# A decode kernel that streams its caches: another start address for values and weights, and a reordered last key step

## The chip, the cores and the metric

The kernel runs on one core of a Trainium2 chip. The metric is the device time of one execution in microseconds; lower is better. Before the change the median of three runs is 195.03 us (194.61 to 195.13). A profiled execution has a span of 192.2 us from its first to its last instruction.

A core has five engines that run beside each other: TensorE (PE in the profile, with its weight loads as PEld), VectorE (DVE), ScalarE (ACT), GpSimd (POOL) and SyncE (SP). Each runs its own instructions in order and waits for the others through semaphores. Sixteen DMA engines move data between the chip's memory (HBM) and the on-chip memory (SBUF), which has 128 partitions. TensorE writes into PSUM.

## The reference

One token goes through attention over a sliding window of cached keys and values, and through a gating branch. Cut to what matters:

```python
x  = layernorm(A_x)                          # (1, 1, 512)
q  = (x @ wq).reshape(32 heads, 128)
k  = k_cache[:, last 4096]                   # 32 heads x 4096 x 128, bf16
v  = v_cache[:, last 4096]
p  = softmax(q . k * 128 ** -0.5)            # per head, over 4096 positions
s  = concat(p @ v) @ wo                      # (4096,) @ (4096, 512)
# gating branch on the same x: g = silu(x1 + gelu(layernorm(x1) @ w3) @ w4),
# where x1 = x + hs, and hs = shifted(h) @ w2 is zero for one token
out = A_x + s * g
```

Every key and every value is used once, for one query. So there is little arithmetic per byte: 32 MiB of K and 32 MiB of V are read, and with the weights the profile counts 79.02 MB.

## The kernel before

The heads go through in eight groups of four (`G = 4`). A group's K is one tile of 128 partitions by 32,768 bytes (4 MiB), and so is its V. Step `s` works on the keys of group `s` and on the values of group `h = s - 2`; steps 8 and 9 have values only.

Memory in a partition is handed out pool after pool, in 32-byte units, so that what is allocated first sets the start of what follows:

```python
k_pool = ctx.enter_context(tc.tile_pool(name="k", bufs=K_BUFS))       # 3 tiles of 32 KiB
kt_pool = ...; prod_pool = ...
const = ctx.enter_context(tc.tile_pool(name="const", bufs=1))         # neg_half lies here
small = ctx.enter_context(tc.tile_pool(name="small", bufs=1))
ps_misc = ctx.enter_context(tc.tile_pool(name="ps_misc", bufs=1, space=PSUM))   # one PSUM bank
ps_tr = ctx.enter_context(tc.tile_pool(name="ps_tr", bufs=3, space=PSUM))
# ... other PSUM pools, and sm_pool for the softmax's small tiles
small.tile([P, 96], BF16, name="pad")
wts_guard = tc.tile_pool(name="wts", bufs=1)    # wq, w2, w3, w4; given up at step 2
# at step 2, in the same place:
v_pool = ctx.enter_context(tc.tile_pool(name="v", bufs=V_BUFS))       # 2 tiles of 32 KiB
wo_blk[2] = v_pool.tile([P, 4, D], BF16, tag="wo_4", bufs=1, name="wo_4")
wo_rows = v_pool.tile([P, H - h_part, D], BF16, tag="wo_rows", bufs=1, name="wo_rows")
# at step 5, in one of the three K buffers:
wo_24 = k_pool.tile([P, 32, D], BF16, tag="kv", name="wo_24")
```

As compiled, the three K tiles start at bytes 16,512, 49,280 and 82,048 of a partition, wq at 151,680, w2 at 184,448, w3 at 188,544, w4 at 199,552, and the two V tiles at 159,872 and 192,640. All of these are 128 more than a multiple of 256. The constant `neg_half` starts at 130,208.

The scores of a group are computed in two ways at once. VectorE multiplies 64 or 80 of the 128 key columns by the query and sums (`k_vector`, four parts). The others go over TensorE: `keys(b0, b1)` turns batches of eight columns (`k_turn`: four transposes, and a copy by ScalarE) and multiplies them by the query (`k_scores`). Then the maximum is taken, and the exponentials:

```python
def sm_max(g):      # VectorE: gather the scores, maximum of each partition
    nc.vector.tensor_reduce(out=s["S"][:, n:CP], in_=s["own"][:, 0:CP - n, :], axis=AX.X, op=ALU.add)
    nc.vector.tensor_reduce(out=s["m1"][:], in_=s["S"][:], axis=AX.X, op=ALU.max)

def sm_turn(g):     # TensorE turns the maxima into a row (in ps_misc); VectorE reduces it
    nc.tensor.transpose(mt_ps[:], s["m1"][:], ident_f[:])
    nc.vector.tensor_reduce(out=mx[:], in_=mt_ps[:].rearrange(...), axis=AX.X, op=ALU.max)
    nc.vector.tensor_scalar(out=md[0:1, :], in0=mx[:], scalar1=-scale, ...)

def sm_exp(g):      # TensorE spreads it to all partitions (ps_misc); ScalarE: four exponentials
    nc.tensor.matmul(mb_ps[:], lhsT=par_t[:]..., rhs=md[:], start=True, stop=True)
    nc.scalar.copy(out=mb[:], in_=mb_ps[:])
    for a in range(G):
        nc.scalar.activation(out=s["pT"][:, :, a], in_=s["S"][:], func=ACT.Exp, scale=scale,
                             bias=mb[:, a:a + 1], accum_out=s["sum"][:, a:a + 1])
```

The values: `v_wide` multiplies a group's V by its weights (32 matmuls, then a copy to SBUF by ScalarE), `v_turn` turns the result (four transposes, in ps_misc, or in ps_tr for the last group), `v_add` and `v_out` sum it and divide by the denominator (VectorE). Then the output projection, in blocks of 16, 8, 4 and 4 heads: `ox_spread` and `ox_pick` bring a block into the form that `y_wide` needs. `y_open` takes a ps_tr bank and clears it, and `y_wide` multiplies the heads by the rows of wo.

The engines' programs in the last steps, in order:

```python
            # step 7 (last keys)
            k_vector(s, kn, 0); keys(0, 2)
            v_turn(h - 1); v_add(h - 1); v_out(h - 1)
            k_vector(s, kn, 1); keys(2, 4)
            sm_den(h); sm_rden(h)
            keys(4, nb - 1)                 # nb is 8 here
            sm_turn(s - 1)
            keys(nb - 1, nb)
            k_scores(s, nb - 1); sm_own(s)
            k_vector(s, kn, 2)
            v_wide(h, v)                    # h = 5: the sixth V
            sm_exp(s - 1)
            k_vector(s, kn, 3)
            sm_max(s); sm_turn(s)           # the last maximum
            v_turn(h); v_add(h); v_out(h)
            ox_spread(1)
            y_open(); y_wide(0, False)
            # step 8
            ox_pick(1)
            sm_exp(NG - 1)
            y_wide(1, False)
            sm_den(NG - 2); sm_rden(NG - 2)
            v_wide(h, v)                    # h = 6: the seventh V
            # ...
            # step 9: the eighth V, loaded in four parts, used part by part (v_wide, v_part);
            # the last four heads with their own rows of wo (y_head), and the end
```

The loads are issued by SyncE in program order as soon as their buffers are free. The last V goes into the buffer of the sixth, and the last four rows of wo (`wo_rows`) are loaded after it.

Of the kernel before, what the change touches and what calls it, by code (L numbers as in the profile page):

```python
# [8 lines left out]
P = 128  # L9
BF16 = mybir.dt.bfloat16  # L10
FP32 = mybir.dt.float32
ACT = mybir.ActivationFunctionType
ALU = mybir.AluOpType
# [13 lines left out]
def kernel(  # L27
# [14 lines left out]
    nc = tc.nc  # L42
# [20 lines left out]
    const = ctx.enter_context(tc.tile_pool(name="const", bufs=1))  # L63
# [54 lines left out]
    nc.vector.tensor_copy(out=sel[:], in_=ident_bf[:, 0:P:32].unsqueeze(1).to_broadcast([P, PB, G]))  # L118
    ind = const.tile([P, 1], FP32, name="ind")
    nc.vector.tensor_reduce(out=ind[:], in_=ident_f[:, 0:P:32], axis=AX.X, op=ALU.max)  # L120
    neg_half = const.tile([P, 1], FP32, name="neg_half")
    nc.vector.memset(neg_half[:], -0.5)


# [33 lines left out]
    def ln_stats(src_f, tag):  # L158
        ps = ps_misc.tile([P, KC], FP32, tag="misc", name="ln_ps")
        nc.tensor.matmul(ps[:], lhsT=ones_f[:], rhs=src_f, start=True, stop=True)  # L160
        tot = small.tile([P, 1], FP32, name=f"ln_tot_{tag}")
        nc.vector.reduce_sum(out=tot[:], in_=ps[:], axis=AX.X)
        negmean = small.tile([P, 1], FP32, name=f"ln_negmean_{tag}")
        nc.vector.tensor_scalar(out=negmean[:], in0=tot[:], scalar1=-1.0 / D,
                                scalar2=None, op0=ALU.mult)
        xc = small.tile([P, KC], FP32, name=f"ln_xc_{tag}")
        nc.vector.tensor_scalar(out=xc[:], in0=src_f, scalar1=negmean[:], scalar2=None,
                                op0=ALU.add)
        sq = small.tile([P, KC], FP32, name=f"ln_sq_{tag}")
        nc.vector.tensor_tensor(out=sq[:], in0=xc[:], in1=xc[:], op=ALU.mult)  # L170
        ps2 = ps_misc.tile([P, KC], FP32, tag="misc", name="ln_ps2")
        nc.tensor.matmul(ps2[:], lhsT=ones_f[:], rhs=sq[:], start=True, stop=True)
        vtot = small.tile([P, 1], FP32, name=f"ln_vtot_{tag}")
        nc.vector.reduce_sum(out=vtot[:], in_=ps2[:], axis=AX.X)
        rstd = small.tile([P, 1], FP32, name=f"ln_rstd_{tag}")
        nc.vector.tensor_scalar(out=rstd[:], in0=vtot[:], scalar1=1.0 / D,
                                scalar2=LN_EPS, op0=ALU.mult, op1=ALU.add)
        nc.gpsimd.tensor_tensor(out=rstd[:], in0=rstd[:], in1=neg_half[:], op=ALU.pow)
        return xc, negmean, rstd


# [86 lines left out]
    for i, (col, w) in enumerate(terms):  # L268
# [28 lines left out]
                            op=ALU.max)  # L297
# [19 lines left out]
    def k_vector(g, kn, part):  # L317
        m = nd(g) // 4
        rows = slice(m * part, m * part + m)
        prod = prod_pool.tile([P, 20, Dh], BF16, tag="prod", name="prod")  # L320
        nc.vector.tensor_tensor(out=prod[:, 0:m, :], in0=kn[:, rows, :],  # L321
                                in1=q_bc[:, g:g + 1, :].to_broadcast([P, m, Dh]), op=ALU.mult)
        nc.vector.tensor_reduce(out=st[g]["S"][:, rows], in_=prod[:, 0:m, :], axis=AX.X, op=ALU.add)  # L323
# [37 lines left out]
    def sm_max(g):  # L361
        s = st[g]
        n = nd(g)
        nc.vector.tensor_reduce(out=s["S"][:, n:CP], in_=s["own"][:, 0:CP - n, :], axis=AX.X, op=ALU.add)  # L364
        s["m1"] = sm_pool.tile([P, 1], FP32, tag="m1", name="m1")
        nc.vector.tensor_reduce(out=s["m1"][:], in_=s["S"][:], axis=AX.X, op=ALU.max)  # L366
# [11 lines left out]
    def sm_exp(g):  # L378
        s = st[g]
        mb_ps = ps_misc.tile([P, G], FP32, tag="misc", name="mb_ps")  # L380
        nc.tensor.matmul(mb_ps[:], lhsT=par_t[:].rearrange("k b a -> k (b a)"), rhs=md[:], start=True,  # L381
                         stop=True)
        mb = sm_pool.tile([P, G], FP32, tag="mb", name="mb")
        nc.scalar.copy(out=mb[:], in_=mb_ps[:])  # L384
        s["pT"] = sm_pool.tile([P, CP, G], BF16, tag="pT", name="pT")
        s["sum"] = sm_pool.tile([P, G], FP32, tag="sum", name="sum")
# [3 lines that stand above are left out]
# [112 lines left out]
    def y_open():  # L502
        yr[0] = ps_tr.tile([P, KC, P], FP32, tag="pt", name="yr_ps")
        zeros(yr[0][:])
# [18 lines left out]
    for s in range(NG + LAG):  # L523
        h = s - LAG
        last = h == NG - 1
        kn = load_kv(k_pool, A_k_cache, s, (0, 64, CP) if s == 0 else (0, CP)) if s < NG else None
        if s == LAG:
            wts_guard.__exit__(None, None, None)
            v_pool = ctx.enter_context(tc.tile_pool(name="v", bufs=V_BUFS))
            wo_blk[2] = v_pool.tile([P, 4, D], BF16, tag="wo_4", bufs=1, name="wo_4")  # L530
            wo_rows = v_pool.tile([P, H - h_part, D], BF16, tag="wo_rows", bufs=1, name="wo_rows")
        if last:
            v = load_kv(v_pool, A_v_cache, h, cuts)
            for r, n in ((H - G, 2), (H - 2, 1), (H - 1, 1)):
                load_rows(r, n)
        elif h >= 0:
            v = load_kv(v_pool, A_v_cache, h)
        if h == 3:
            wo_24 = k_pool.tile([P, 32, D], BF16, tag="kv", name="wo_24")
            wo_blk[0], wo_blk[1] = wo_24[:, 0:16, :], wo_24[:, 16:24, :]  # L540
            load_wo(0)
        if h == 5:
            load_wo(1)
            load_wo(2)

        if s < NG:
            nb = len(batches(s))

            def keys(b0, b1):
                for b in range(b0, b1):  # L550
                    k_turn(s, kn, b)
                    if b > 0:
                        k_scores(s, b - 1)

            k_open(s)
            k_vector(s, kn, 0)
            keys(0, 2)
            if s == 7:
                v_turn(h - 1)
                v_add(h - 1)  # L560
                v_out(h - 1)
            elif s > 1:
                sm_den(s - 2)
                sm_rden(s - 2)
            elif s == 1:
                sm_max(0)
            k_vector(s, kn, 1)
            keys(2, 4)
            if s == 7:
                sm_den(h)  # L570
                sm_rden(h)
                keys(4, nb - 1)
                sm_turn(s - 1)
                keys(nb - 1, nb)
            else:
                if s > 0:
                    sm_turn(s - 1)
                keys(4, nb)
            k_scores(s, nb - 1)
            sm_own(s)  # L580
            if s == 7:
                k_vector(s, kn, 2)
                v_wide(h, v)
                sm_exp(s - 1)
                k_vector(s, kn, 3)
                sm_max(s)
                sm_turn(s)
                v_turn(h)
                v_add(h)
                v_out(h)  # L590
                ox_spread(1)
                y_open()
                y_wide(0, False)
                continue
            if s > 0:
                sm_exp(s - 1)
            if h > 0:
                v_turn(h - 1)
            k_vector(s, kn, 2)
            if h >= 0:  # L600
                v_wide(h, v)
            if h > 0:
                v_add(h - 1)
                v_out(h - 1)
            if s == 6:
                ox_spread(0)
            k_vector(s, kn, 3)
            if s == 6:
                ox_pick(0)
            if s > 0:  # L610
                sm_max(s)
        elif s == NG:
            ox_pick(1)
            sm_exp(NG - 1)
            y_wide(1, False)
            sm_den(NG - 2)
            sm_rden(NG - 2)
            v_wide(h, v)
            sm_den(NG - 1)
            sm_rden(NG - 1)  # L620
            v_turn(h)
            v_add(h)
            v_out(h)
            ox_spread(2)
        else:
            v_open(h)
            v_wide(h, v, cuts[1])
            ox_pick(2)
            v_turn(h)
            v_add(h)  # L630
            y_wide(2, True)
            nc.scalar.copy(out=y_sum[:], in_=yr[0][:].rearrange("p j n -> p (j n)"))
            v_part(h, v, cuts[1], cuts[2])
            rows_add(y_ps, ind, y_sum, False)
            for c0, c1 in zip(cuts[2:], cuts[3:]):
                v_part(h, v, c0, c1)
            v_out(h)
            for r in range(H - G, H):
                y_head(r)
# [36 lines left out]
```

## Time and profile before

| view | value |
|---|---|
| median of three runs | 195.03 us |
| span of the profiled execution | 192.2 us |
| moved by DMA | 79.02 MB, mean 411 GB/s over the span |
| VectorE busy | 151.1 us (79%) |
| TensorE matmul busy | 116.9 us (61%) |
| ScalarE busy | 89.3 us (46%) |
| mean granted TensorE clock | 0.711 |

How to read it: the page's second part cuts the span into 40 equal slices, 4.8 us each. A digit is the busy share of an engine in a slice in tenths, PEclk the granted clock of TensorE in tenths, DMA the mean busy share of the 16 DMA engines, and the last line what they moved. The chain of waits follows the end of the span back, at each step to what released it. A line of the timeline has the start, the duration, the engine, the source line, output and inputs, and in brackets how long the engine sat idle before it and what ended that.

The busiest groups of instructions have the number of instructions, their busy time, the mean of one in ns, and the idle time before them:

```profile
L323 DVE TENSOR_REDUCE S<-prod 128x20 f32<-128x2560 bf16 (+1 forms) x32 | 86.0, 2686 | 1.1
L342 ACT COPY kt<-pt 128x1024 bf16<-128x1024 bf16 x52 | 51.2, 1012 | 40.4 <-PE pt L339 38.8
L372 PE MATMUL mt_ps<-ident_f,m 128*1 128x128 f32 x8 | 2.8, 346 | 21.3 <-DVE rden L399 17.1
```

### The profile page before, as it was taken

What the parts mean: (1) busy time and instruction counts of PE and PEld (TensorE: products, weight loads), DVE (VectorE), ACT (ScalarE), POOL (GpSimd) and SP (SyncE); (2) the same over time, 40 slices, a digit from 0 to 9 for tenths busy, and PEclk for the clock granted to TensorE, in tenths of its full rate; (3) what the DMA queues carried; (4) which work ended last, traced back from release to release, by engine and by line L of the source; (5) the groups of instructions that cost most, each with busy time, mean ns of one, the idle gap of its engine ahead of it and who ended that gap; (6) DMA issues with size and microseconds to landing.
All of it is one profiled execution on the core that took longest, in us unless ns stands there. A gap on an engine that the chain in (4) does not pass through costs nothing.

```text
span 192.2 us, 2877 instructions
## 1 busy us (share of the span) xinstructions
PE 116.9 (61%) x1177; PEld 74.5 (39%) x1177; DVE 151.1 (79%) x175; ACT 89.3 (46%) x191; POOL 2.3 (1%) x11
## 2 busy tenths in 40 slices
PE   1653854988734368256846772690988089629972
PEld 0430222767523334143335341540862076312451
DVE  1660159979999999999999999998999997972111
ACT  2001370887894176437454564642575049722320
POOL 2110000000000000000000000000000000000000
PEclk9999696556955557955695588557566858965795
DMA  6999999999999999999999999999999999999990
GB/s 210 452 430 401 417 423 433 436 436 428 436 431 436 436 419 436 430 436 436 426 436 423 430 426 399 453 430 426 423 436 431 433 436 389 477 430 389 409 355 20
DMA packets 4733, 79.02 MB, mean 411 GB/s; under 512 B 657, under 2 KB 1265, under 8 KB 1777
## 3 DMA queue, kind: packets, MB, share of 16 engines
q1 hardware_dynamic: 4424, 74.65, 91.5%
q10 hardware_dynamic: 296, 4.20, 5.1%
q8 instruction: 9, 0.15, 0.3%
q14 instruction: 4, 0.02, 0.0%
HBM read 78.84 MB, written 0.00 MB: 410 GB/s over the span
## 4 chain that ended last, share of the span: by engine, by line
DVE 46%; DMA 43%; PE 4%; ACT 3%; SPq 1%; issue 1%; ACTq 0%; DVEq 0%
DMA kv<-in_A_k_cache_dram 31%; DVE S L323 28%; DVE prod L321 15%; DMA kv<-in_A_v_cache_dram 9%; ACT kt L342 3%; DMA x_bf<-in_A_x_dram 2%; PE pt L339 2%; SPq L76 1%; PE ov L427 1%; DVE m L366 1%; DVE S L364 1%; DVE mx L374 1%; PE ot_ps L442 0%; PE sT L350 0%; DVE md L376 0%
## 5 line engine op out<-in xcount | busy, mean ns | idle before, releaser
L323 DVE TENSOR_REDUCE S<-prod 128x20 f32<-128x2560 bf16 (+1 forms) x32 | 86.0, 2686 | 1.1
L342 ACT COPY kt<-pt 128x1024 bf16<-128x1024 bf16 x52 | 51.2, 1012 | 40.4 <-PE pt L339 38.8
L339 PE MATMUL pt<-ident_f,kv 128*128 128x128 f32 x208 | 45.9, 371 | 11.1 <-DMA kv<-in_A_k_cache_dram 11.1
L321 DVE TENSOR_TENSOR prod<-kv,q_bc 128x2560 bf16<-128x2560 bf16 (+1 forms) x32 | 45.4, 1417 | 4.1 <-DMA kv<-in_A_k_cache_dram 3.9
L339 PEld LDWEIGHTS pt<-ident_f,kv 128*128 128x128 f32 x208 | 33.6, 193 | 14.9 <-DMA kv<-in_A_k_cache_dram 10.6
L350 PE MATMUL sT<-q_pair,kt 128*128 128x8 bf16 x416 | 19.4, 170 | 15.6 <-ACT kt L342 15.3
L350 PEld LDWEIGHTS <-kt 128*128 128x128 bf16 x416 | 16.3, 104 | 26.7 <-ACT kt L342 25.8
L427 PE MATMUL ov<-kv,pT 128*16 128x512 bf16 x240 | 22.7, 544 | 0.0
L372 PE MATMUL mt_ps<-ident_f,m 128*1 128x128 f32 x8 | 2.8, 346 | 21.3 <-DVE rden L399 17.1
L388 ACT ACTIVATE pT<-S,mb 128x128 bf16<-128x128 f32 x32 | 14.0, 575 | 0.3
L431 ACT COPY ov_sb<-ov 128x512 f32<-128x512 f32 x8 | 4.7, 586 | 16.8 <-PE ov L427 16.8
L427 PEld LDWEIGHTS <-pT 128*16 128x16 bf16 x240 | 6.7, 113 | 11.7 <-issue 10.3
L359 ACT ACTIVATE own<-sT,par 128x48 f32<-128x48 f32 (+1 forms) x32 | 7.5, 356 | 3.7 <-PE sT L350 3.7
L442 PE MATMUL ot_ps<-ident_f,ov_sb 128*128 128x128 f32 x32 | 7.5, 378 | 2.7 <-ACT mb L384 1.4
L372 PEld LDWEIGHTS mt_ps<-ident_f,m 128*1 128x1 f32 x8 | 0.6, 80 | 21.7 <-DVE rden L399 17.4
L211 DVE CAST q_row<-qr_ps 128x512 bf16<-128x512 f32 x1 | 0.7, 692 | 10.2 <-PE qr_ps L208 10.2
L388 ACT ACTIVATION_READ_ACCUMULATOR pT<-S,mb 128x1 f32 x32 | 8.3, 261 | 0.0
L381 PE MATMUL mb_ps<-md,par_t 5*128 5x4 f32 x16 | 3.9, 311 | 4.1 <-DVE md L376 3.8
L442 PEld LDWEIGHTS ot_ps<-ident_f,ov_sb 128*128 128x128 f32 x32 | 4.8, 188 | 3.6 <-ACT mb L384 1.8
L255 ACT ACTIVATE a_row<-a_ps 128x384 bf16<-128x384 f32 x1 | 0.5, 491 | 12.0 <-remote 12.0
L208 PE MATMUL qr_ps<-wq_sb,xq_bf 128*1 128x512 bf16 x32 | 3.4, 608 | 3.7 <-DMA wq_sb<-in_A_wq_dram 3.7
L384 ACT COPY mb<-mb_ps 128x4 f32<-128x4 f32 x8 | 1.3, 168 | 9.2 <-PE mb_ps L381 9.2
(120 smaller groups left out, 82.3 us busy)
## 6 DMA issues: line engine op xcount, KB each, us to landing
kv<-in_A_k_cache_dram SPq DMA_DIRECT2D x7, 4096.0 KB, 29.5
kv<-in_A_v_cache_dram SPq DMA_DIRECT2D x7, 4096.0 KB, 31.4
wq_sb<-in_A_wq_dram ACTq DMA_DIRECT2D x1, 4096.0 KB, 17.6
kv<-in_A_k_cache_dram SPq DMA_DIRECT2D x2, 2048.0 KB, 25.6
wo<-in_A_wo_dram SPq DMA_DIRECT2D x1, 2048.0 KB
kv<-in_A_v_cache_dram SPq DMA_DIRECT2D x1, 2048.0 KB
w_sb<-in_B_w_dram SPq DMA_DIRECT2D x1, 1376.0 KB, 9.2
w_sb<-in_B_w_dram SPq DMA_DIRECT2D x1, 1280.0 KB, 19.3
```

The lines of the kernel that those rows point to most:

```text
L208: nc.tensor.matmul(qr[b][32 * a:32 * a + 1], lhsT=xq_bf[:, c:c + 1], rhs=wc[:, 4 * b:4 * b + 4, a, :], start=False, stop=(c == KC - 1), sk ...
L321: nc.vector.tensor_tensor(out=prod[:, 0:m, :], in0=kn[:, rows, :], in1=q_bc[:, g:g + 1, :].to_broadcast([P, m, Dh]), op=ALU.mult)
L323: nc.vector.tensor_reduce(out=st[g]["S"][:, rows], in_=prod[:, 0:m, :], axis=AX.X, op=ALU.add)
L339: nc.tensor.transpose(pt[:, i, :], kn[:, c:c + 2, :].rearrange("p c d -> p (c d)").bitcast(FP32), ident_f[:])
L342: nc.scalar.copy(out=kts[b][:, 0:n, :], in_=pt[:, 0:n, :].bitcast(BF16))
L350: nc.tensor.matmul(st[g]["sT"][:, c:c + 2, :].rearrange("p c a -> p (c a)"), lhsT=kt[:, i, l::2], rhs=q_pair[:, g, l, :], start=(l == 0), ...
L359: nc.scalar.mul(s["own"][:, 0:m, a], s["sT"][:, 0:m, a], par[:, a:a + 1])
L381: nc.tensor.matmul(mb_ps[:], lhsT=par_t[:].rearrange("k b a -> k (b a)"), rhs=md[:], start=True, stop=True)
L388: nc.scalar.activation(out=s["pT"][:, :, a], in_=s["S"][:], func=ACT.Exp, scale=scale, bias=mb[:, a:a + 1], accum_out=s["sum"][:, a:a + 1])
L427: nc.tensor.matmul(ov[r:r + 4 * G], lhsT=s["pT"][:, c:c + 4, :].rearrange("p i a -> p (i a)"), rhs=v[:, c:c + 4, :], start=(i < 4), stop=( ...
L431: nc.scalar.copy(out=s["ov_sb"][:], in_=ov[:])
L442: nc.tensor.transpose(ot_ps[:, step * j:step * j + P], s["ov_sb"][:, j, :], ident_f[:])
```

## The change

It has two parts that touch different things.

The first makes `neg_half`, a constant of which one column is used, 33 columns wide. It then takes 132 bytes, which is 160 with the rounding, in place of 32. Everything that is allocated after it starts 128 bytes later. The K tiles come ahead of it and stay. The aim is that the V tiles and the weights start at multiples of 256 bytes.

The second reorders the last key step. The transpose of the seventh group's maxima goes one batch of keys ahead. The turning of the sixth V's result, the opening of the output bank and the first block's products come before the last `k_vector` part, the last maximum comes at the end of the step, and its transpose moves into step 8, behind `ox_pick(1)`. The aim is that TensorE has this work where it would wait for the maximum.

```diff
-    neg_half = const.tile([P, 1], FP32, name="neg_half")
+    neg_half = const.tile([P, 33], FP32, name="neg_half")
     nc.vector.memset(neg_half[:], -0.5)
...
-        nc.gpsimd.tensor_tensor(out=rstd[:], in0=rstd[:], in1=neg_half[:], op=ALU.pow)
+        nc.gpsimd.tensor_tensor(out=rstd[:], in0=rstd[:], in1=neg_half[:, 0:1], op=ALU.pow)
...
             if s == 7:
                 sm_den(h)
                 sm_rden(h)
-                keys(4, nb - 1)
+                keys(4, nb - 2)
                 sm_turn(s - 1)
-                keys(nb - 1, nb)
+                keys(nb - 2, nb)
...
                 k_vector(s, kn, 2)
                 v_wide(h, v)
                 sm_exp(s - 1)
+                v_turn(h)
+                y_open()
+                y_wide(0, False)
                 k_vector(s, kn, 3)
-                sm_max(s)
-                sm_turn(s)
-                v_turn(h)
                 v_add(h)
                 v_out(h)
                 ox_spread(1)
-                y_open()
-                y_wide(0, False)
+                sm_max(s)
                 continue
...
         elif s == NG:
             ox_pick(1)
+            sm_turn(NG - 1)
             sm_exp(NG - 1)
             y_wide(1, False)
```

## The prediction

> **What bounds the kernel now.** I first read the page's slices of the span: the row of DMA shares says whether the load stream ever pauses.
>
> ```profile
> DVE  1660159979999999999999999998999997972111
> DMA  6999999999999999999999999999999999999990
> GB/s 210 452 430 401 417 423 433 436 436 428 436 431 436 436 419 436 430 436 436 426 436 423 430 426 399 453 430 426 423 436 431 433 436 389 477 430 389 409 355 20
> ```
>
> The reader is to see two full rows: VectorE is at nines from about 30 us to 160 us, the DMA engines from 5 us to the end. Only one of them can set the time. The chain of waits, second, gives 46% to VectorE and 43% to DMA, but its last part names only loads and their consumers:
>
> ```profile
> 130.49 23.55 DMA kv<-in_A_k_cache_dram
> ...
> 167.34 0.26 SPq L76
> ...
> 168.94 18.23 DMA kv<-in_A_v_cache_dram
> 187.17 0.04 issue
> 187.22 0.60 PE oT L459 x16
> ...
> 188.06 0.78 PE y_ps L155 x16
> ```
>
> VectorE's chain ends in a wait for the seventh K (0.78 us at 134.63), so all its work before that had caught up with the loads. The third view, busy time by stage, shows the stream's rate:
>
> ```profile
> 42.00:134.00 92.00, 53.19 (x540) 35.66 (x539) 90.58 (x69) 50.96 (x118) 0.00 (x0) 0.67 1.01 431
> 134.00:187.00 53.00, 38.00 (x406) 23.75 (x406) 37.87 (x48) 24.17 (x54) 0.00 (x0) 0.73 0.99 419
> ```
>
> The last two columns are DMA share and GB/s: the share is 1.01 and 0.99 (packets are counted where they start), so no transfer waits for a buffer long enough to leave the engines idle. I checked this at the last place where it could: the last V is issued at about 167 us, when the buffer of the sixth comes free, and the V ahead of it in the queue keeps the engines busy to 177 us. In the trace's packet records one 4 MiB K or V takes 9.7 us. So the loads, end to end, set the time. The fourth view, the last stage in order of time, shows that what is left of TensorE's lag is gone before the end:
>
> ```profile
> 178.11 2.86 PE L427 MATMUL ov<-kv,pT 128*16 128x512 bf16 x32
> 182.26 1.04 PE L427 MATMUL ov<-kv,pT 128*16 128x512 bf16 x16
> 187.22 0.59 PE L459 MATMUL oT<-pT,kv 128*128 128x4 bf16 x16 [0.47 <-DMA kv<-in_A_v_cache_dram]
> ```
>
> The landing records put the seventh V at 177.38 us, so TensorE starts on it 0.7 us late (178.11). The first part of the eighth lands at 182.13 and TensorE is there at 182.26, 0.1 us late. For the last part (landing 187.17) it waits 0.47 us. The last four output-projection matmuls start at 188.54, after the last weight row lands at 188.50. From there to the end of the span are 3.7 us, the output's store above all.
>
> [...] the packets are equally long beside busy and idle engines, so moving compute about should leave the stream alone.
>
> **The change part by part.**
>
> 1. The addresses. Neg_half grows from 4 to 132 bytes, so all that is allocated after it moves by 128. In the compiled kernel before, K tiles start at 16,512, 49,280 and 82,048, wq at 151,680, the V tiles at 159,872 and 192,640; all are 128 past a multiple of 256. K lies ahead of neg_half and stays there; so does the large output-weight block that reuses a K buffer. Wq, w2, w3, w4, the V tiles and the late output weights come to multiples of 256. Packets that become aligned: V 7 x 128 + 4 x 128 = 1,408; wq, w2, w3 and w4 128 each plus w4's rest 96, that is 608; wo_4 128 and wo_rows 512. Sum 2,656, or 166 on each of 16 engines. [...] VectorE, ScalarE and TensorE read the moved tiles at the same element steps; I count nothing for them.
>
> 2. The seventh maximum's transpose goes ahead by one batch of keys. VectorE sits idle 1.31 us before the reduction at 163.26, for a TensorE transpose at 162.96 that stands behind a batch which ScalarE copies out in 1.0 us. One batch earlier gives VectorE back about 1.0 us: its last reduction ends near 169.7 instead of 170.7.
>
> 3. The sixth V's turning (4 transposes, 1.11 us), the zeroing (0.63) and the first block's 16 products (1.88) go ahead of the last maximum. TensorE sits idle 4.23 us before the transpose at 171.55; these 3.6 us now lie in that idle stretch. On VectorE the adds, product and spread (0.23 + 0.16 + 0.23) go ahead of the maximum (0.41 + 0.29). The maximum's transpose now comes behind the second block's pick. With VectorE ready at 169.7: 0.6 of adds, 0.7 of maximum, 0.5 of pick, then transpose 0.4, two small reductions 0.5 and the broadcast 0.6, so ScalarE can start the last exponentials at about 173 us instead of 176.75. Then TensorE takes the seventh V as it lands (177.4 instead of 178.11). Worth at the end: nothing directly, since TensorE waited 0.47 us for the last V part already. It is slack that keeps TensorE with a stream which would finish up to 0.8 us earlier; without it a shorter stream would be partly lost at 182.26.
>
> Sum: 0 to 0.78 us from part 1, 0 from 2 and 3, with 0.1 us either way from the tail's clock (granted 1.0 from 180.1 to 186.9, then 0.5; where those steps fall can change).
>
> **The rivals.** (a) Fixed overhead: the stream is as long as before, the reordering lands in idle time, and the time is 195.0. For it: the 4-byte and 256-byte packets, and K and V packets that are equally long. [...] (b) The alignment term is real: 194.25. (c) Skew between the engines is what matters: the last landing's sixteen parts come from 186.63 to 188.50, six engines being almost 2 us ahead. The 32 KiB packets take 1213, 1218 or 1221 ns, and if the slower ones are an effect of the start address, the gain could be 5 to 8 ns a packet, 0.8 to 1.3 us in all, 193.7 to 194.2. Against it: wq has the same address residue and mostly 1213. (d) The reordering costs: the single buffer that the transposes, broadcasts and sums share now serves in another order, and a wait there could delay the last exponentials past 177.4; it would take a delay of more than 4 us from my 173, so I give this little. It would make 195.5 or more. (e) TensorE's reordered 3.6 us delay the eighth key step's own maximum or the release of the V buffer: the release comes from the products of the sixth V, which stand ahead of all that is moved, so no.
>
> **Range and chances.** I give (a) some 55%, (b) 30%, (c) 8%, (d) and the unforeseen 7%. The mean of 195.0, 194.25, 193.95 and 195.6 by these is 194.73; I predict 194.7. The runs before spread over 0.5 us, so the range is 193.9 to 195.4. Two per cent are 3.9 us. No part can bring that, as the stream's bytes do not change; none should cost it. Chances: faster 0.01, within 0.98, slower 0.01.
>
> **What would show it.** Part 1: [...] a last landing near 187.7 instead of 188.50. If they stay, (a) is right. Part 2: VectorE's idle before the maximum at step seven falls from 1.31 to about 0.3 us. Part 3: TensorE's idle of 4.23 us is filled, ScalarE's wait of 7.3 us before the last broadcast ends at about 173, and the seventh V's products start with its landing. I would be wrong if DMA share fell below 0.99 anywhere after 10 us, if a product waited for something other than a landing after 182 us, or if the packets of K, which don't move, changed.

## The result, and the profile after

The changed kernel takes 193.62 us (median of five, 193.59 to 193.77) against 195.0 us (194.61 to 195.13): a ratio of 0.9937, interval 0.9923 to 0.9952. The time is 1.4 us shorter, below the predicted range. The profiled executions took 194.46 us before and 193.61 us after, so the two profiles hold 0.85 us of it. In every ratio and group of times below, executions more than 1.5% above the fastest of their kernel are left out.

The page's slices of the changed kernel, the granted clock of TensorE, DMA share and GB/s:

```profile
PEclk9999589555855558955695588555566855588795
DMA  6999999999999999999999999999999998999990
GB/s 209 449 418 417 422 428 435 438 438 430 438 433 438 431 428 431 438 438 432 421 432 438 425 421 408 442 438 435 431 438 440 435 431 377 486 421 387 420 367 28
```

DMA still works through: packets are counted where they start, so the slice that reads 8 stands before one of 486 GB/s. The commonest reading of a slice is 438 GB/s where it was 436: the stream is the same, a little denser. The end of its chain of waits (start, duration, what):

```profile
171.40 14.92 DMA kv<-in_A_v_cache_dram
186.32 0.04 issue
186.36 0.60 PE oT L459 x16
...
187.20 0.76 PE y_ps L155 x14
```

The last V lands at 186.32 instead of 187.17. What follows is as long as before. The last row of weights lands at 187.62 instead of 188.50. So in this profile the whole gain has arrived before the last 4 us. Before the change, TensorE sat idle for 4.23 us ahead of the transpose of the last maximum:

```profile
171.55 0.37 PE L372 MATMUL mt_ps<-ident_f,m 128*1 128x128 f32 x1 [4.23 <-DVE m L366]
```

TensorE in the last stage of the changed kernel, in order of time:

```profile
169.40 0.38 PE L381 MATMUL mb_ps<-md,par_t 5*128 5x4 f32 x2
...
172.52 0.27 PE L372 MATMUL mt_ps<-ident_f,m 128*1 128x128 f32 x1 [0.32 <-DVE pick L490]
...
176.60 3.26 PE L427 MATMUL ov<-kv,pT 128*16 128x512 bf16 x32 [1.95 <-DMA kv<-in_A_v_cache_dram]
...
181.44 1.04 PE L427 MATMUL ov<-kv,pT 128*16 128x512 bf16 x16 [0.23 <-DMA kv<-in_A_v_cache_dram]
...
186.36 0.59 PE L459 MATMUL oT<-pT,kv 128*128 128x4 bf16 x16 [0.46 <-DMA kv<-in_A_v_cache_dram]
```

The reader is to see the brackets: TensorE now waits for the seventh V (1.95 us), for the first part of the eighth (0.23) and for its last part (0.46), where before only the last of these was a wait for a load. The idle 4.23 us ahead of the transpose are down to 0.32.

The DMA packets changed as follows (the trace's packet records; 32 KiB packets of K and V without the few above 1240 ns; below the table, the time of all packets divided by 16 engines):

```
32 KiB packets     1213-1215   1216-1219   1220+   mean ns   K mean   V mean
before                44%         32%       24%    1216.9    1216.9   1216.9
changed               83%         11%        7%    1214.1    1214.9   1213.3

DMA packet time per engine, all sizes: before 186.46 us, changed 185.68 us
```

Over 90% of the V packets now took 1213 ns. Packets of 8 KiB fell from 313.6 to 309.0 ns in the mean, those of 1 KiB only from 46.9 to 46.0. K packets, whose tiles had not moved, became shorter too.

### The profile page after: what moved, and what is told of

It reads as the page before. It is cut to its first block, busy times and chain, and to the rows that moved or that the text cites. A ratio compares the mean times of both kernels' runs of the same rounds, so it can differ in the third digit from the quotient of the medians.

```text
span 191.4 us, 2877 instructions
## 1 busy us (share of the span) xinstructions
PE 119.9 (63%) x1177; PEld 77.5 (40%) x1177; DVE 151.2 (79%) x175; ACT 89.5 (47%) x191; POOL 2.3 (1%) x11
## 4 chain that ended last, share of the span: by engine, by line
DVE 46%; DMA 41%; PE 8%; ACT 1%; SPq 1%; issue 1%; DVEq 0%; ACTq 0%
DMA kv<-in_A_k_cache_dram 31%; DVE S L323 28%; DVE prod L321 15%; DMA kv<-in_A_v_cache_dram 8%; PE pt L339 3%; DMA x_bf<-in_A_x_dram 2%; PE ov L427 2%; ACT kt L342 1%; PE sT L350 1%; SPq L76 1%; DVE m L366 1%; DVE S L364 1%; DVE mx L374 1%; PE ot_ps L442 0%; DVE md L376 0%
## 5 line engine op out<-in xcount | busy, mean ns | idle before, releaser
L339 PE MATMUL pt<-ident_f,kv 128*128 128x128 f32 x208 | 48.2, 385 | 10.5 <-DMA kv<-in_A_k_cache_dram 10.5
L339 PEld LDWEIGHTS pt<-ident_f,kv 128*128 128x128 f32 x208 | 35.3, 201 | 14.0 <-DMA kv<-in_A_k_cache_dram 10.1
L350 PEld LDWEIGHTS <-kt 128*128 128x128 bf16 x416 | 16.9, 106 | 26.4 <-ACT kt L342 25.2
L427 PE MATMUL ov<-kv,pT 128*16 128x512 bf16 x240 | 25.0, 591 | 2.2 <-DMA kv<-in_A_v_cache_dram 2.2
L427 PEld LDWEIGHTS <-pT 128*16 128x16 bf16 x240 | 7.5, 121 | 15.2 <-issue 14.7
L399 DVE RECIPROCAL rden<-den_ps 128x4 f32<-128x4 f32 x8 | 1.4, 175 | 6.7 <-PE den_ps L394 6.7
```

The costliest lines, as they stand in the source:

```text
L339: nc.tensor.transpose(pt[:, i, :], kn[:, c:c + 2, :].rearrange("p c d -> p (c d)").bitcast(FP32), ident_f[:])
L350: nc.tensor.matmul(st[g]["sT"][:, c:c + 2, :].rearrange("p c a -> p (c a)"), lhsT=kt[:, i, l::2], rhs=q_pair[:, g, l, :], start=(l == 0), ...
L427: nc.tensor.matmul(ov[r:r + 4 * G], lhsT=s["pT"][:, c:c + 4, :].rearrange("p i a -> p (i a)"), rhs=v[:, c:c + 4, :], start=(i < 4), stop=( ...
```

## The experiments

Each kernel is compared with the kernel before on its own chip. On the chips used here the times of the kernel before lie in two groups, 194.3 and 195.0 to 195.1 us, about two thirds of its executions in the lower, and most of the other kernels have two as well. A median can then jump by which group it falls into, so I give the median of each group, with the number of executions in it, beside the ratio over all of them.

**1. The addresses alone.** The kernel before with the first two hunks only (the first is shown):

```diff
-    neg_half = const.tile([P, 1], FP32, name="neg_half")
+    neg_half = const.tile([P, 33], FP32, name="neg_half")
```

> The changed kernel minus its reordering: only neg_half is widened, so V tiles and weights start at multiples of 256 and every engine's program is that of the kernel before. Theory A (the gain is the load stream's: packets into unaligned tiles often take 1216 to 1222 ns in place of 1213, and aligned ones don't): V packets at 1213 ns, last landing near 187.6 us of the span, and nearly the whole gain, 193.6 to 193.9 us; up to 0.3 us is lost again because TensorE comes late to the seventh V as in the kernel before. Theory B (the reordering carries the gain, the packets are a side effect): 194.7 us or more.

Measured: ratio 0.9968 (0.9955 to 0.9982), median 193.93 us. The 22 times run from 193.31 to 194.58 us and show no two groups; no gap between neighbours is over 0.17 us. V packets 1213.4 ns, last V landing 186.18 us. The stream got its whole gain. But the profiled execution took 194.48 us; its TensorE:

```profile
178.50 3.59 PE L427 MATMUL ov<-kv,pT 128*16 128x512 bf16 x32
...
183.37 1.04 PE L427 MATMUL ov<-kv,pT 128*16 128x512 bf16 x16
...
187.29 0.96 PE L459 MATMUL oT<-pT,kv 128*128 128x4 bf16 x32
...
188.50 0.39 PE L155 MATMUL y_ps<-wo_rows,o 128*1 128x128 bf16 x16 [0.26 <-DVE o L469]
```

No bracket names a load. The landings are at 176.40 (seventh V) and 181.24 (first part of the eighth), and TensorE is 2.1 us late for both. The last two parts of V are taken in one go, since both have landed, and the output products start at 188.50, after the last row has lain there since 187.47. In this execution the shorter stream is lost to a late TensorE. The addresses carry the gain (theory A): the ratio is clear of 1, and the median lies just above the 193.6 to 193.9 us expected. The 0.3 us I allowed for lateness was too little.

**2. The order alone.** The changed kernel with `neg_half` one column wide.

> The changed kernel minus its addresses: reordered, with neg_half one column wide, so V and weights are 128 past a multiple of 256. Theory A: the work moves into idle time and the load stream stays as long, 194.9 to 195.1 us, V packets spread over 1213 to 1222 ns as before. Theory B: 193.6 to 194.0 us.

Measured: ratio 1.001 (0.9988 to 1.0031), groups 194.33 (11) and 195.85 us (3). V packets 1216.8 ns, last V at 186.95 us. No gain. Theory B falls.

**3 and 4. K too, and K alone.** Both put 128 bytes in front of the K pool:

```diff
+    front = ctx.enter_context(tc.tile_pool(name="front", bufs=1))
+    front.tile([P, 64], BF16, name="front_pad")
     k_pool = ctx.enter_context(tc.tile_pool(name="k", bufs=K_BUFS))
```

The first also has `neg_half` back at one column, so that K, V and weights are all at multiples of 256; the second keeps 33, so that K is and V and weights are not.

> The changed kernel with 128 bytes put in front of the K pool and neg_half one column wide again: K, V, weights and the output-weight block in a K buffer all start at multiples of 256. Theory A: the excess that remains in the changed kernel (3 to 4.5 ns a packet in the first three K loads, the output-weight block and the seventh K, some 0.2 us on each engine in sum) goes too: 193.3 to 193.5 us, all large packets at 1213 or 611 ns. Theory C (only the pattern of V and weights matters, K's packets are slowed by something else, such as the HBM side): K's packets stay as in the changed kernel and the time is 193.6 us.

> The changed kernel with 128 bytes put in front of the K pool: K tiles start at multiples of 256, V tiles and weights are 128 past one again. Theory A in its plain form (a packet pays for its own tile's start only): K packets at 1213 ns, V packets spread as before, and about half of the gain, 194.2 to 194.5 us. Theory D (the excess is not the packet's own, it builds up among unaligned loads that follow each other and needs time to come back, since K packets between aligned V's were nearly clean in the changed kernel): V packets mostly clean as well, 193.8 to 194.1 us.

Measured: all at 256, ratio 0.9973 (0.9952 to 0.9994), groups 193.28 (13) and 194.87 us (8), 99% of the 32 KiB packets at 1213 to 1215 ns, last V at 185.95 us. K alone, ratio 0.9985 (0.9957 to 1.0014), groups 193.70 (6) and 195.14 us (3), so unclear in time; its profile has 97% of the packets at 1213 to 1215 ns, V's among them (mean 1213.4), and the last V at 186.42 us.

So K's packets are slowed by their start address as V's are: theory C falls. And the excess isn't a packet's own: V packets off a multiple of 256 are nearly clean when K loads on one lie between them, as K packets mostly were between aligned V loads in the changed kernel. What theory D expected of the packets came; that the excess builds up and needs time to come back is not shown. In the changed kernel the excess stays where loads off a multiple of 256 (off-boundary loads) follow each other, in the first three K (1216.6 ns in the third), and in the seventh K (1216.6), which comes behind the weight block in a K buffer.

**5. The changed kernel again.**

> The changed kernel as it is, beside the runs that follow on the same chip. Here the kernel before has two groups of times, some 0.9 us apart, so the lower group is compared. Theory A with TensorE's lateness: addresses alone gained 0.3% and the order alone nothing, but both together gain 0.6 to 0.8%, 193.2 to 193.6 us, because the reordering lets TensorE keep up with the shorter stream. Theory E (the two parts just add up): 0.3%, 193.7 us.

Measured: ratio 0.9953 (0.9938 to 0.9967), 193.54 us, all five executions in the lower group; the kernel before in the same comparison 194.31 (29) and 195.07 us (10). The time lies in the range expected of theory A. The gain, 0.47% over all executions and 0.40% from lower group to lower group, lies between that theory's 0.6 to 0.8% and theory E's 0.3%. So this run does not decide whether the order adds to the addresses, and run 11 is less favourable.

**6 and 7. Other starts.** `neg_half` 17 columns wide, and 9: V and weights at 192 and at 160 past a multiple of 256.

> The changed kernel with neg_half 17 columns wide: V tiles and weights start at 192 past a multiple of 256 (a multiple of 64 only), K at 128. Theory A1 (any start off a multiple of 256 gives the same now-and-then excess): V packets spread over 1213 to 1222 ns, mean 1217, and 194.2 to 194.4 us. Theory A2 (the smaller the common power of two, the worse): V packets above 1222 ns in the mean and a time over 195 us.

> The changed kernel with neg_half 9 columns wide: V tiles and weights start at 160 past a multiple of 256 (a multiple of 32 only), K at 128. Theory A1: as with 192, V packets of 1217 ns in the mean and 194.2 to 194.4 us. Theory A2: longer packets than with 192, and slower still.

Measured: 192, ratio 1.0032 (1.0013 to 1.0052), groups 194.44 (8) and 195.72 us (11), V packets 1217.1 ns; 160, ratio 1.0021 (1.0004 to 1.0038), groups 194.32 (14) and 195.68 us (8), V packets 1216.7 ns. The last V lands at 186.95 and 186.97. All three off-boundary starts (128, 160, 192) give nearly the same mean: for the packets A1 holds and A2 falls. Of the starts tried, only those on a multiple of 256 have the shorter mean. The single packets do differ: at 192 half of V's take 1215 ns and 4% take 1213, where 24% did in the kernel before.

In time, A1 was not met at 192, whose median is 195.62 us. Both kernels are the reordered one with the excess left in, and both are slower than the kernel before, by 0.3 and 0.2%, with intervals clear of 1. Their upper groups and that of the order alone (195.68 to 195.85 us) lie 0.6 to 0.8 us above the kernel before's on the same chips (195.06 and 195.07). So without a shorter stream the new order seems to cost a little in some executions; the order alone, with 14, is too few to show it by itself.

**8 and 9. The loads alone**, at 128 and at 256. All computation and the rows of wo are left out (code cut):

```python
    for s in range(NG + LAG):
        h = s - LAG
        if s < NG:
            ks[s] = load_kv(k_pool, A_k_cache, s)
        # at s == LAG: the weights' pool is given up for v_pool
        if h >= 0:
            v = load_kv(v_pool, A_v_cache, h)
            see(v[:, 0, 0:1])          # VectorE copies one column
        if s < NG:
            see(ks[s][:, 0, 0:1])
```

> Loads alone: x, wq, w2, w3, w4, then the eight K and the first eight V tiles in the order of the kernel before, three K and two V buffers, all 128 past a multiple of 256. It leaves out all the computation (VectorE reads one column of each tile so that its buffer comes free) and the rows of wo, and its output is not the reference's. Theory F (the excess belongs to the DMA writes and their addresses): packets of 32 KiB spread over 1213 to 1222 ns, mean near 1217, as beside the full computation. Theory G (it comes from engines that read and write the memory at the same time): all at 1213 ns.

> The same loads alone with all tiles at multiples of 256. Both theories: packets at 1213 ns. Theory F: the last V lands 0.7 to 1.3 us earlier than in the run with 128; theory G: at the same time.

One execution each: 181.27 and 180.51 us. From the pages, at 128 and then at 256:

```profile
span 179.5 us, 109 instructions
## 1 busy us (share of the span) xinstructions
DVE 3.5 (2%) x24; POOL 0.4 (0%) x5
```

```profile
span 178.7 us, 109 instructions
## 1 busy us (share of the span) xinstructions
DVE 3.5 (2%) x24; POOL 0.4 (0%) x5
```

```
32 KiB packets     1213-1215   1216-1219   1220+   mean ns
loads at 128          38%         38%       24%    1217.1
loads at 256          99%          1%        0%    1213.1
```

With TensorE and ScalarE idle and VectorE nearly so, the excess is as large as beside the full computation (mean 1217.1 ns, 1216.9 in the kernel before), and 0.76 us go with it. Theory F holds: it goes with the addresses that the loads are written to (1213.1 ns at 256). It also puts aside a rival to the runs above, that the shift moved the engines' own small tiles too.

The profiles of the whole kernel say the same of the end of the stream. With V off a multiple of 256 and K at 128 (before and runs 2, 6 and 7) the last V lands at 186.95 to 187.17 us; in the changed kernel and with its addresses alone (four profiles) at 186.18 to 186.32. The means are 187.01 and 186.25, which is 0.76 us again.

**10 and 11. All at 256 against the changed kernel.**

> The changed kernel with K at multiples of 256 as well, again, beside the changed kernel on one chip. The lower group of its times at 193.1 to 193.4 us, 0.2 to 0.3 us under the changed kernel's, because the last V lands 0.3 us earlier; an upper group near 194.8 us in some executions, where TensorE is granted half its clock in the last 17 us and can't keep up with the stream.

> The changed kernel again, the other half of the comparison. 193.4 to 193.7 us; if TensorE's granted clock decides on the upper group here too, some executions near 194.8 us, otherwise none.

Measured: all at 256, ratio 0.9981 (0.9961 to 1.0001), groups 193.29 (9) and 194.79 us (10); changed, ratio 0.9987 (0.9965 to 1.0009), groups 193.55 (15) and 195.32 us (7). The changed kernel has an upper group too, and with it its gain can't be told from none over all executions. This run's profile is of the upper group (195.16 us). The row of TensorE's clock, and its last stage:

```profile
PEclk9999997596855556655985575558587669695555
```

```profile
176.58 3.59 PE L427 MATMUL ov<-kv,pT 128*16 128x512 bf16 x32 [3.39 <-DMA kv<-in_A_v_cache_dram]
...
182.08 1.89 PE L427 MATMUL ov<-kv,pT 128*16 128x512 bf16 x16
...
184.65 1.12 PE L442 MATMUL ot_ps<-ident_f,ov_sb 128*128 128x128 f32 x4 [0.56 <-ACT ov_sb L431]
...
187.71 1.01 PE L459 MATMUL oT<-pT,kv 128*128 128x4 bf16 x32
188.98 0.59 PE L155 MATMUL y_ps<-wo_rows,o 128*1 128x128 bf16 x16 [0.26 <-DVE o L469]
```

Same program and same landings as in the profile above (seventh V 176.54, last part 186.31), but the last four slices have the clock at 0.5, where that one has 0.8, 0.7 and 0.9 before the last. The first part of the eighth V takes 1.89 us instead of 1.04, a turning 1.12 instead of 0.66, and the output products start 1.78 us later (188.98 for 187.20). Before 176 us TensorE had 3.39 us to spare; this work can't start until the seventh V has landed. The profile of run 6 (195.59 us) is of an upper group too and ends alike: the clock at 0.5 in the last four slices, the output products at 189.41, 1.0 us after the last row of weights landed.

**12 and 13. The seventh V in halves**, on the changed kernel and with all at 256:

```diff
-            v = load_kv(v_pool, A_v_cache, h)
+            v = load_kv(v_pool, A_v_cache, h, (0, 64, CP) if h == NG - 2 else (0, CP))
```

> The changed kernel with the seventh V loaded in two halves, so that TensorE can start on the first half some 4.8 us before the second lands. Theory T (the upper group of times is TensorE late behind the loads when it is granted half its clock in the last 17 us): at half clock TensorE is done with the seventh V some 1.8 us earlier, the upper group of 195.0 to 195.3 us vanishes or comes down below 194.3, and the lower one stays at 193.4 to 193.6 us. Theory H (the half clock itself, or something that goes with it, delays the end whatever is done before): the upper group stays near 195.1 us in a third of the executions.

> The same with K at multiples of 256 too. Theory T: nearly all executions at 193.1 to 193.4 us, under both the kernel before and the changed one. Theory H: half of them near 194.8 us as without the split.

Measured: ratio 0.9989 (0.9973 to 1.0005) with groups 193.74 (6) and 194.59 us (16), and 0.9984 (0.9969 to 0.9998) with groups 193.35 (3) and 194.23 us (17). The upper group comes down from 195.32 to 194.59 and from 194.79 to 194.23, but more executions fall into it. (The kernel before's own groups differ by under 0.1 us between these comparisons.) From the first one's profile, an execution of 193.58 us:

```profile
181.29 1.04 PE L427 MATMUL ov<-kv,pT 128*16 128x512 bf16 x16 [2.44 <-DMA kv<-in_A_v_cache_dram]
...
183.02 1.11 PE L442 MATMUL ot_ps<-ident_f,ov_sb 128*128 128x128 f32 x4 [0.57 <-ACT ov_sb L431]
```

TensorE now waits 2.44 us for the eighth V, where it was 0.7 us late in the execution of run 11 and waited 0.23 us in the changed kernel's first profile; what comes after then runs as long as at half clock (a turning of 1.11 us; 1.12 in run 11, 0.66 in the changed kernel's first profile). Work taken out of the last 10 us lowers the upper group, as theory T says, but not to the 194.3 us expected of the first, and not to nearly all executions in the lower group. Neither version is better than the changed kernel beyond doubt. The shortest lower group is that of all at 256, which in run 10 was 0.26 us under the changed kernel's (193.29 against 193.55 us).

## Why the prediction was wrong

Two of its steps failed. One is the 0.78 us of part 1, a fixed time that each packet was to lose with an aligned start: the author's estimate, which no trace showed. The most frequent packet times stayed (46 ns at 1 KiB, 1213 at 32 KiB), and what the address costs is an excess over them, which the chances had at 8%. The other is the base: the median that the sum started from, and the claim that TensorE's lag is gone before the end. The stream's 0.85 us alone would have given 194.2 us, inside the range.

**The bound: right in these two profiles.** The load stream sets the end, and the stream's change shows in the landings one for one: the last landing came 0.88 us earlier, the profiled time is 0.85 us shorter. Where TensorE runs the tail at half clock it can set the end instead: in run 11, at 0.5 in the last four slices, the output products start 1.4 us after the last row of weights has landed.

**Part 1, the addresses: the grounds failed, the size was near.** The step, with rivals (a) and (b), asked whether a constant part of every packet's time would shrink with an aligned start: 0.78 us over 166 packets on an engine, or nothing. That figure was the author's estimate and is not shown by any trace. The records of the kernel before show the constant part itself (most frequent time of a packet; 32,768 bytes: wq):

```
bytes        4    256   1024   4096   10240   32768
took, ns     9     18     46    159     385    1213
```

From 1024 to 32,768 bytes these rise by 37.6 ns per KiB. By an estimate from that slope, each of the six sizes has 8.4 to 8.9 ns on top, the 4-byte packets too, as (a) had it. This part stayed: in the changed kernel all 608 packets of 1 KiB take 46 ns, where 497 did before, and the most frequent time at 32 KiB is still 1213. What the address costs lies on top, in the packets of 1216 to 1222 ns that I had seen in the before's records and put at 8% as rival (c). It is not one time that each off-boundary packet pays: in the kernel before 44% of the K and V packets are at 1213 to 1215 ns, others at 1218 and 1221. Nor does its mean follow the distance from the multiple of 256: 1216.9, 1216.7 and 1217.1 ns at 128, 160 and 192. In place of the estimate stands a fall of 0.78 us in packet time per engine, of which 0.52 us are excesses under 40 ns and the rest rarer, longer ones. The longer ones differ nearly as much between two executions with the same addresses (1.55 us per engine before, 1.36 with the order alone), so the address's own share may be nearer 0.5, which leaves some 0.25 of the 0.76 us at the landings unexplained. That the sum equals my figure to the digit is chance. K packets, which don't move, became shorter by 2 ns in the mean: I had named that as a sign of being wrong, and it came. My argument against (c) was that wq has the same residue and 1213 ns. The runs showed that an off-boundary load can be nearly clean beside aligned ones. Why wq is clean with K and V at 128 is not shown; on a multiple of 256 its packets were no shorter (1213.9 ns, 1213.2 before). With the moved tiles VectorE and ScalarE worked as long as before: busy for 151.1 and 151.2 us, and for 89.3 and 89.5.

**Part 2, the seventh transpose: right at the same clock.** VectorE's idle time before that reduction fell from 1.31 to 1.15 us, not to 0.3. But in the changed profile TensorE runs this stretch at half its clock (0.50 from 158 to 166 us, against 0.90 before). Like must be set beside like. The kernel before, and then the order alone (clock 0.89):

```profile
163.26 0.28 DVE L374 TENSOR_REDUCE mx<-mt_ps 1x4 f32<-1x128 f32 x1 [1.31 <-PE mt_ps L372]
162.21 0.28 DVE L374 TENSOR_REDUCE mx<-mt_ps 1x4 f32<-1x128 f32 x1 [0.48 <-PE mt_ps L372]
```

The addresses alone, where the transpose is not moved, and then the changed kernel (both 0.50):

```profile
163.65 0.28 DVE L374 TENSOR_REDUCE mx<-mt_ps 1x4 f32<-1x128 f32 x1 [2.30 <-PE mt_ps L372]
162.65 0.28 DVE L374 TENSOR_REDUCE mx<-mt_ps 1x4 f32<-1x128 f32 x1 [1.15 <-PE mt_ps L372]
```

The move is worth 0.83 us at nearly full clock and 1.15 us at half, about the 1.0 predicted. It didn't matter for the time.

**Part 3, the reordering: right in its course.** The idle 4.23 us were filled, ScalarE's last broadcast came at 173.8 (predicted 173), and the seventh V's products started 0.04 us after it landed. "Worth at the end: nothing directly" fits the order alone (1.001), while runs 6 and 7 point to a small cost, which rival (d) had at 7% and through another wait. That a shorter stream can need the slack is shown by one profile of the addresses alone, late by 1 us at the output products. What the order adds to the addresses in time is not shown: the medians are 193.93 us without it and 193.54 to 193.67 with it, but on different chips, the ratios overlap (0.9968 against 0.9937, 0.9953 and 0.9987), and the slowest executions with it (to 196.03 us) are slower than any without (194.58).

**The base: the step that missed 0.5 us.** "What is left of TensorE's lag is gone before the end" was read from one profile of 194.46 us, and its margin was 0.1 us at 182.26. The median I predicted from was 195.03, half a microsecond above that profile, and I took it for the same execution. In the runs above the kernel before has two groups 0.7 to 0.8 us apart; three of its five times on record are 195.0 or more, and none of the changed kernel's five is above 193.77. So the recorded 1.4 us are about 0.85 of stream and some 0.5 of how many executions had a late TensorE. The first is shown. The second is argued from the times: upper executions were profiled for the changed kernel and for its version at 192, none for the kernel before. I also gave the tail's clock 0.1 us either way, and it was worth 1.78 us at the output products in the two profiles of the changed kernel.

**Still open:** why aligned loads clear the off-boundary loads between them, why four in ten off-boundary packets pay next to nothing, what sets the pattern of TensorE's clock, and whether the new order is worth keeping. The lower groups, which hold the stream's part, agree over the comparisons of runs 5 and 11: 194.3 us before, 193.5 to 193.6 changed.

## What to carry to other kernels

Where a trace shows DMA share at 1.0 to the end, look at the spread of packet times and not only at their base: here a start on a multiple of 256 bytes took 4 ns off 1217 and 0.8 us off the last landing, and with every large tile on one the lower group of times came down by a further 0.26 us. How much of it reaches the median depends on the end of the kernel: the changed kernel's ratio was 0.9937, 0.9953 and 0.9987 in three comparisons. A shorter stream only pays if the engine that follows it can keep up: with the addresses alone the last V landed at 186.18 us instead of 187.17, and the profiled execution took 194.48 us against 194.46. Check that margin at half of TensorE's clock, and compare two profiles' stages only where they had the same clock (the same turning took 0.66 us in one profile of the changed kernel and 1.12 in the other). And see whether the profile you reason from took the median time, before you add its parts to that median.

## What was not expected of the hardware

- What an off-boundary load pays depends on the loads around it. V tiles at 128 past a multiple of 256 had 1216.9 ns beside K tiles at 128, and 1213.4 ns beside K tiles at 0.
- Starts at 128, 160 and 192 past a multiple of 256 were about equally slow in the mean: 1216.9, 1216.7 and 1217.1 ns.
- The same program with the same landings ended 1.55 us apart (193.61 and 195.16 us) by where TensorE's half clock fell.
